# The maxima of a sliding-window attention, laid out in scratch as a transpose leaves them, with a new order of one unit's transfers

## Chip, cores and metric

The kernel runs on one NeuronCore of a Trainium2 chip. The metric is the device time of one execution in microseconds. The core has a matrix engine (PE, with its weight loads as PEld), a vector engine (DVE), a scalar engine (ACT), GpSimd (POOL) and a sync engine (SP) which here issues nearly all the DMA transfers. Each engine works through its own instructions in order; semaphores tie them to each other.

## What is computed

Two branches over the same input `x` (2048 tokens, 512 features, float32), mixed by a sigmoid gate per token:

```python
def _A_ref(x, wqkv, wo):          # H = 32 heads of 16, window W = 256
    q, k, v = ...                 # x @ wqkv, split in heads
    scores = einsum("bhqd,bhkd->bhqk", q, k) * (Dh ** -0.5)
    scores = where(0 <= query - key < W, scores, -1e9)
    p = softmax(scores, axis=-1)
    return einsum("bhqk,bhkd->bhqd", p, v)... @ wo

def _B_ref(x, w_gate, w_up, w_down):
    return (sigmoid(x @ w_gate) * (x @ w_up)) @ w_down

g = sigmoid((x * gate_w).sum(-1, keepdims=True))
return g * _A_ref(...) + (1 - g) * _B_ref(...)
```

## The kernel before

**Number format.** Every float32 operand is split in a high and a low part (ACT rounds the high one, DVE subtracts), and three products replace one.

**Units.** Heads go in 8 groups of 4, tokens in 16 blocks of 128; the main loop (line 779) runs over units u, one block of one head group each, 128 in all (`NU`), and a tail of ten more. Four units make a step s (512 tokens of a head group, 32 in all), two steps a stack t of the ring.

**The ring.** For scores the kernel keeps stacked operands in a ring of three (`ring`, line 101): per head 64 rows that hold the parts of q and of k, in four slots along the second axis: slots 0 and 1 for q (heads 0 and 1 of a group in slot 0, heads 2 and 3 in slot 1), slots 2 and 3 for k. Row 0 of each 32 is the place where -max of a query is put, as a high and a low part in two groups of rows, so that the second score product comes out with the maximum subtracted already. `stack_build` (line 281) lists a stack's transfers: a fill that puts zeros in the rows of the maxima, eight of the high parts (`ring<-sh`) and four of the low (`ring<-sl`). They are put on SP four at a time, in four units from u = 8k+1 on (`sdma[:SD]`, line 799).

**Two passes of scores.** In unit u, for each of the group's four heads, `s_part` (line 314) forms the scores with the queries on partitions, and DVE takes each query's masked maximum (`mxs`). `LAG` = 9 units later `st_part` (line 366) forms them again, transposed, with keys on partitions and the maximum subtracted; ACT takes the exponential into `pbuf`, and GpSimd masks it. `st` of unit u reads queries of up to two blocks ahead of block u-9.

**The maxima's way.** After the four units of a step DVE negates and splits the maxima (`max_split`, line 337) into `nm`, 128 queries on partitions by 32 columns (head, part, block), and transposes it in 32x32 squares into `nt`: partition (a, h, l, b), 32 columns t, where a is the quarter of the 128 queries. `max_store` (line 347) sends it to DRAM in four transfers, one for each a, so that the scratch is laid out (h, l, b, query); `max_load` (line 353) reads it into the ring with one transfer: four destination partitions, two slots, runs of 512 floats.

**Visits.** From u = 13 (`PVLAG`) on, every fourth unit is a visit: before its first scores, the product of the exponentials with the values (`pv_part`, line 400) of a finished step runs; six key blocks as a rule, four for the first step of a head group (u = 13, 29, 45, ...). In a visit step (u-5)//4 is also split and stored. ACT copies the product out (`o_take`, line 417) in the visit's first slot, and lists five stores of it: four to `oT_scratch`, one of the sums. Visits are at u = 13, 17, 21, ...; every second one (17, 25, ... 113) is also the unit in which a stack's transfers begin.

**Order on SP.** SP's order is the order of the program. At the start of a unit `run_dmas(later)` issues the stores listed before it, then up to four transfers of a stack go; in a visit the four stores of the maxima follow inside the unit. The load of the maxima comes in the unit after the visit (`u % 4 == 2`, line 803), behind that unit's `later` and its share of the stack. Loads of weights and stores of gate and up products (`gu_scratch<-sp`, by `later`) stand among these.

**Filler work and held projections.** Between the score products the matrix engine does the projections of q and k (`pj`), then the gate and up products (`gu`), by a generator of turns. ACT and DVE work that follows is kept in lists: `evac` (one a slot, first), `acts` (one a slot if `evac` is empty), `behind` (DVE). A finished projection is copied to a buffer (`pr`, from the same four buffers, tag `sp`, that the gate and up products are copied to) and its split is put in `held` until the unit that line 821 names.

Of the kernel before, what the change touches and what calls it, by code (L numbers as in the profile page):

```python
# [7 lines left out]
F32 = mybir.dt.float32  # L8
# [6 lines left out]
P = 128  # L15
# [5 lines left out]
HG = 4  # L21
NG = H // HG
CH = 512
NC = T // CH
# [15 lines left out]
PVLAG = LAG + 4  # L40
SD = 4
QB = 32
# [15 lines left out]
def gated_mix_kernel(  # L58
# [11 lines left out]
    nc = tc.nc  # L70
# [21 lines left out]
    rec_d = nc.dram_tensor("rec_scratch", (NC, H, CH), F32, kind="Internal").ap()  # L92
    gu_d = nc.dram_tensor("gu_scratch", (2, NFM, P, T), F32, kind="Internal").ap()
    tail_d = nc.dram_tensor("tail_scratch", (NB, P, 2 * TF), F32, kind="Internal").ap()
    max_d = nc.dram_tensor("max_scratch", (NG * NC, HG, 2, 4, P), F32, kind="Internal").ap()
    fill_d = nc.dram_tensor("fill_scratch", (2, CH2), F32, kind="Internal").ap()

    cpool = ctx.enter_context(tc.tile_pool(name="cpool", bufs=1))
# [14 lines left out]
    NU = NG * NB  # L113
# [22 lines left out]
    with ExitStack() as actx:  # L136
# [159 lines left out]
        def run_dmas(dmas):  # L296
            for dst, src in dmas:
                nc.sync.dma_start(dst, src)  # L298
# [36 lines left out]
        nms = {}  # L335

        def max_split(s):
            mx = mxs.pop(s)
            nm = spool.tile([P, HG, 2, 4], F32R, tag="nm", name=f"nm{s}", bufs=1)
            nc.vector.tensor_scalar(nm[:, :, 0], mx, -1.0, None, op0=ALU.mult)  # L340
            nc.vector.scalar_tensor_tensor(
                nm[:, :, 1], mx, -1.0, nm[:, :, 0].bitcast(F32), op0=ALU.mult, op1=ALU.subtract,
            )
            nms[s] = spool.tile([P, QB], F32, tag="nt", name=f"nt{s}")
            nc.vector.transpose(nms[s], nm.bitcast(F32).rearrange("p h l b -> p (h l b)"))

        def max_store(s):
            nt = nms.pop(s)
            dst = max_d[s].rearrange("h l b (a t) -> a (h l b) t", t=QB)
            for a in range(P // QB):  # L350
                nc.sync.dma_start(dst[a], nt[a * QB:(a + 1) * QB])

        def max_load(s):
            st = ring[s // 2 % RING].bitcast(F32).rearrange("(a r) j f -> r a j f", r=QB)
            o = s % 2 * CH
            nc.sync.dma_start(
                st[0, :, 0:2, o:o + CH], max_d[s].rearrange("(p s) l b t -> (s l) p (b t)", p=2),
            )

        homes = (((0, 1), (9, 1), (3, 2), (4, 2)), ((0, 1), (3, 1), (9, 2), (10, 2)))  # L360

# [33 lines left out]
        later = []  # L395
# [102 lines left out]
        def gu_mm(f, c, w, k, half=None, second=False):  # L498
            if (f, c, w) not in gp:
                gp[f, c, w] = ps.tile([P, CH], F32, tag="misc", name=f"gu{f}_{c}_{w}", bufs=3)  # L500
            return group_mm(gp[f, c, w], gv[:, 0, w], gv[:, 1, w], c, k, half, second)
# [51 lines left out]
        def proj_post(s):  # L553
            proj_hi(s)
            behind.append(lambda: proj_lo(s))
# [41 lines left out]
        def proj_sum(s):  # L597
# [12 lines left out]
                lambda k, h=None, x=False, a=(f, c, w): gu_mm(*a, k, h, x),  # L610
# [9 lines left out]
        held = []  # L620
# [139 lines left out]
        def hold_group(step, _, post):  # L760
            for k in range(3 * ND):
                step(k)
            post()
# [8 lines left out]
        sdma = []  # L772
# [6 lines left out]
        for u in range(N):  # L779
            if u == LAG:  # L780
                vctx.close()
                pctx = ExitStack()
                ppool = pctx.enter_context(tc.tile_pool(name="ppool", bufs=1))
                pbuf = ppool.tile([P, 15, HG, P], F32, name="pbuf")
                pv = ps.tile([P, CH], F32, tag="pv", name="pv", bufs=1)
            if u == 1:
                proj_post(NC)
            if u == 4:
                load_gu(0, 0)
                load_gu(0, 1)  # L790
            if u % 8 == 1 and u > 8 and u // 8 + 1 < NP:
                sdma = stack_build(u // 8 + 1)
            if u % 16 == 8 and u // 16 + 2 < NG:
                raw_q = load_wqk(u // 16 + 2)
            if u in (4, 8, NU):
                max_store(u // 4 - 1)
            run_dmas(later)
            later.clear()
            run_dmas(sdma[:SD])
            del sdma[:SD]  # L800
            if u in (5, LAG):
                max_load(u // 4 - 1)
            if u % 4 == 2 and PVLAG < u < NU:
                max_load(u // 4 - 1)
            if u in WD_LOAD:
                load_d(WD_LOAD[u])
            if u == NU:
                max_load(NSTEP - 1)
            if u in TAIL_LOAD:
                tail_load(TAIL_LOAD[u])  # L810
            if u == WO:
                both = apool.tile([P, ND, CH], F32, tag="w0", name="woraw")
                wo_raw.extend(both[:, d] for d in range(ND))
                nc.sync.dma_start(both, wo.rearrange("(c p) n -> p c n", p=P))
            for s4 in proj_at.get(u, ()):
                if u < LAG:
                    first.insert(0, (
                        lambda k, h, s4=s4: proj_slot(s4, k, h), lambda s4=s4: proj_sum(s4)))
                else:
                    work.append(proj_group(s4))  # L820
            while held and u >= 8 * (held[0][0] // 2) - 11:
                acts.append(held.pop(0)[1])
            if u == N - 1:
                hold_group(*rest.pop(0))
            for hh in range(HG):
                if hh == 0 and u >= PVLAG and (u - PVLAG) % 4 == 0:
                    pv_part((u - PVLAG) // 4)
                    if u < NU:
                        max_split((u - 5) // 4)
                        max_store((u - 5) // 4)  # L830
                if u < NU:
                    s_part(u, hh)
                if 0 <= u - LAG < NU:
                    st_part(u - LAG, hh ^ 1 if u < NU else hh)
                if u < LAG:
                    flush(behind)
                    if hh % 2 == 1:
                        upto = n_first * (2 * u + 1 + hh // 2) // (2 * LAG)
                        run_first(upto - done)
                        done = upto  # L840
                else:
                    dense = u < NU and (u - PVLAG) % 4 == 3 and hh > 0
                    if behind and not dense:
                        behind.pop(0)()
                    if evac:
                        evac.pop(0)()
                    elif acts and not dense and (u < NU or hh % 2 == 1):
                        acts.pop(0)()
                if u >= LAG and (hh % 2 == 1 or u < NU) and ((u - PVLAG) % 4 < 3 or hh < HG - 1):
                    if u < N - 2:  # L850
                        next(slots)
            if u < LAG:
                flush(soon)
            if u == LAG - 1:
                split_gu(0, 0)
                split_gu(0, 1)
            if u in (3, 7, NU - 1):
                max_split(u // 4)
            if u // 16 + 2 < NG:
                if u % 16 == 13:  # L860
                    acts.append(lambda g=u // 16 + 2, r=raw_q: (
                        split_wqk(g, r, 0), behind.append(lambda: split_wqk(g, r, 1))))
            if 0 <= u - LAG < NU:
                mask_p(u - LAG)
            if u in TAIL_SPLIT:
                acts.append(lambda d=TAIL_SPLIT[u]: tail_split(d))
            if WD_LOAD.get(u - 1, 8) < 8:
                acts.append(lambda f=WD_LOAD[u - 1]: split_d(f, True))
            if u in WO_SPLIT:
                acts.extend(lambda d=d: wo_split(d) for d in range(WO_SPLIT[u], WO_SPLIT[u] + 1))  # L870
            if SUMS <= u < N - 1 and (u - SUMS) % 4 == 0:
                sums_load((u - SUMS) // 4)
            if SUMS + 2 <= u and (u - SUMS) % 4 == 2:
                behind.append(lambda c=(u - SUMS) // 4: later.append(sums_invert(c)))
            if u == TREAD:
                tail_reads(0)
            if u >= TREAD:
                tail_read(0, 2)
            for n in H_LOAD.get(u, ()):
                h_load(n)  # L880
            if u == N - 1:
                pctx.close()
                lpool = actx.enter_context(tc.tile_pool(name="lpool", bufs=1))
                spare = [lpool.tile([P, CH], F32, name=f"spare{k}") for k in range(6)]
            if u >= N - 2:
                flush(evac)
                flush(acts)
                flush(behind)
                h_skew(u - N - 1)
# [49 lines left out]
        for n, (c, f) in enumerate(steps):  # L939
# [45 lines left out]
            for t in range(4):  # L985
                r = slice(t * QB, (t + 1) * QB)
                mm(pd[t], lw[r, c], w3[r], start=False, stop=True)
            for t in range(4):
                b = 4 * c + t
# [64 lines left out]
```

## Time and profile before

| | before |
|---|---|
| median of three runs | 805.75 us (804.4 to 807.63) |
| the profiled execution | 799.52 us, of which 797.8 are the span from its first to its last instruction |
| PE busy, of the span | 93% |
| DVE, ACT, POOL busy | 61%, 53%, 21% |
| granted PE clock, mean | 0.972 |
| DMA | 103.64 MB, 94607 packets, of them 44958 under 512 B |

The page is of one execution. Its group rows give line, engine, operation, output and inputs by tile name, count, then busy time, mean duration in ns, and the idle time of the engine before such instructions with what ended it. The timeline gives start, duration, engine, line, operation, and in brackets the idle time before; the DMA rows of SP give the time of the issue, not of the transfer. In the chain of waits a DMA's row runs from its issue to its landing.

### The profile page before, as it was taken

To read this page: it belongs to the slowest core of one execution; us is meant where nothing else is said; L and a number is where in the kernel's file an instruction comes from. 1 tells how busy PE (TensorE), PEld (TensorE's weight loads), DVE (VectorE), ACT (ScalarE), POOL (GpSimd) and SP (SyncE) were. 2 spreads that over 40 slices of the span, in tenths; PEclk is the share of its full clock that TensorE was granted. 3 is DMA by queue.
4 is the path that set the end of the run, shared out by engine and by line. 5 is a ranking of instruction groups with operands and counts; after the bars stand their busy time and mean duration, and the time that the engine had idled before them with its cause. 6 is when DMAs were issued, how large, how long until landed. Compare 5 with 4: busy or idle time off the path is not lost.

```text
span 797.8 us, 17545 instructions
## 1 busy us (share of the span) xinstructions
PE 744.7 (93%) x6298; PEld 614.8 (77%) x6298; DVE 487.9 (61%) x1455; ACT 424.3 (53%) x890; POOL 167.4 (21%) x255
## 2 busy tenths in 40 slices
PE   9999989898898979888798989879989999999998
PEld 7788868686787768777687778767878888888886
DVE  4388756565574656565465756655764676848481
ACT  5424746465574546555464656555547564535341
POOL 6101321232232223222221322232223100000000
PEclk9999999999999999999989999998999999999999
DMA  7342342433535233343424242534257797949451
GB/s 280 96 121 65 99 129 81 114 94 94 140 91 144 86 99 99 97 123 97 126 67 136 76 125 65 159 104 126 75 167 221 203 273 193 254 130 268 116 112 53
DMA packets 94607, 103.64 MB, mean 130 GB/s; under 512 B 44958, under 2 KB 57758, under 8 KB 94520
## 3 DMA queue, kind: packets, MB, share of 16 engines
q1 hardware_dynamic: 94376, 102.40, 45.9%
q8 instruction: 49, 0.80, 0.4%
q14 instruction: 38, 0.31, 0.1%
q10 hardware_dynamic: 144, 0.13, 0.0%
HBM read 45.32 MB, written 31.99 MB: 97 GB/s over the span
## 4 chain that ended last, share of the span: by engine, by line
PE 84%; SPq 7%; DMA 5%; issue 2%; ACT 1%; DVE 1%; DVEq 0%; ACTq 0%
PE gu L252 22%; PE pv L408 10%; PE pj L252 9%; PE s L324 6%; SPq L298 6%; PE tp L543 5%; PE st L373 5%; PE pd L86 5%; PE pd L88 5%; PE pd L87 5%; DMA ring<-max_scratch 4%; PE vh L580 3%; PE pa L86 2%; PE pa L87 2%; PE pa L88 2%; PE vps L446 2%
## 5 line engine op out<-in xcount | busy, mean ns | idle before, releaser
L330 DVE CUSTOM_DVE_ANT_0 junk<-s,mask 128x384 f32<-128x384 f32 (+2 forms) x512 | 271.9, 531 | 207.4 <-PE s L324 151.2
L378 ACT ACTIVATE pbuf<-st 128x384 f32<-128x384 f32 (+2 forms) x512 | 241.4, 477 | 232.1 <-PE st L373 168.1
L252 PE MATMUL gu<-xh,w 64*128 64x512 f32 x1152 | 292.3, 401 | 0.0
L373 PE MATMUL st<-ring 64*128 64x384 f32 (+2 forms) x536 | 173.0, 339 | 46.9 <-DMA ring<-max_scratch 46.9
L252 PE MATMUL gu<-xl,w 64*128 64x512 f32 x576 | 192.0, 399 | 0.0
L384 POOL TENSOR_SCALAR_AFFINE_SELECT pbuf<-pbuf 128x512 f32<-128x512 f32 x128 | 85.1, 665 | 437.5 <-ACT pbuf L378 396.4
L252 PEld LDWEIGHTS gu<-xh,w 64*128 64x128 f32 x1152 | 164.5, 190 | 10.4
L324 PE MATMUL s<-ring 64*128 64x384 f32 (+2 forms) x536 | 167.9, 331 | 0.7 <-DVE mx L330 0.6
L373 PEld LDWEIGHTS st<-ring 64*128 64x128 f32 x536 | 100.0, 192 | 57.3 <-issue 48.4
L324 PEld LDWEIGHTS s<-ring 64*128 64x128 f32 x536 | 98.2, 190 | 18.4 <-issue 4.5
L252 PEld LDWEIGHTS gu<-xl,w 64*128 64x128 f32 x576 | 94.2, 190 | 3.7
L252 PE MATMUL pj<-xh,wqh 64*128 64x512 f32 (+1 forms) x228 | 89.3, 418 | 0.0
L252 PE MATMUL pj<-xl,wqh 64*128 64x512 f32 (+1 forms) x228 | 89.0, 415 | 0.0
L408 PE MATMUL pv<-pbuf,V 128*32 128x384 f32 (+2 forms) x1408 | 84.3, 386 | 0.0
L252 PE MATMUL pj<-xh,wql 64*128 64x512 f32 (+1 forms) x228 | 76.4, 422 | 0.0
L408 PEld LDWEIGHTS pv<-pbuf,V 128*32 128x32 f32 x1408 | 41.5, 110 | 41.1 <-issue 30.7
L390 POOL TENSOR_SCALAR_AFFINE_SELECT pbuf<-pbuf 128x512 f32<-128x512 f32 x112 | 73.0, 652 | 0.0
L86 PE MATMUL pd<-ring,hb 128*128 128x512 f32 x160 | 62.3, 389 | 0.0
L88 PE MATMUL pd<-ring,hb 128*128 128x512 f32 x160 | 62.3, 389 | 0.0
L87 PE MATMUL pd<-ring,hb 128*128 128x512 f32 x160 | 62.2, 389 | 0.0
L82 ACT CAST hb<-V 128x512 fp32r<-128x512 f32 x40 | 24.9, 622 | 56.0 <-DVE V L744 47.8
L252 PEld LDWEIGHTS pj<-xh,wql 64*128 64x128 f32 (+1 forms) x228 | 45.6, 204 | 2.3
(127 smaller groups left out, 1122.9 us busy)
## 6 DMA issues: line engine op xcount, KB each, us to landing
gu_scratch<-sp SPq DMA_DIRECT2D x72, 256.0 KB
V<-gu_scratch SPq DMA_DIRECT2D x36, 512.0 KB
ring<-sh SPq DMA_DIRECT2D x128, 128.0 KB
ring<-sl SPq DMA_DIRECT2D x64, 128.0 KB
guraw<-in_wgu_dram SPq DMA_DIRECT2D x18, 256.0 KB
oT_scratch<-ob SPq DMA_DIRECT2D x128, 32.0 KB
xl<-oT_scratch SPq DMA_DIRECT2D x16, 256.0 KB
V<-in_xT_dram SPq DMA_DIRECT2D x15, 256.0 KB
```

Of the source, the lines that this page charges most:

```text
L86: mm(ps, lh, rh, start=first, stop=False)
L87: mm(ps, lh, rl, start=False, stop=False)
L88: mm(ps, ll, rh, start=False, stop=last)
L252: return mm(pt, (wl if w == 2 else wh)[r, d], (xl if w == 1 else xh)[r, d, c * CH:(c + 1) * CH], start=k == 0 and not second, stop=k == 3 ...
L298: nc.sync.dma_start(dst, src)
L324: mm(pt[:, (k - k0) * P:(e - k0) * P], lhsT, blk(g, k, hh, 1, e - k), start=k == k0, stop=e == i + 1, skip_group_check=True,)
L330: nc.vector.tensor_tensor_reduce(junk[:, 0:n], pt[:, 0:n], mask[:, 3 * P - n:], scale=1.0, scalar=NEG, op0=ALU.add, op1=ALU.max, accum_out ...
L373: mm(pt[:, (q - j) * P:(e - j) * P], lhsT, blk(g, q, hh, 0, e - q), start=q == j, stop=e == last, skip_group_check=True,)
L378: exps.append(nc.scalar.activation(p_blk(u, hh, 0, n), pt[:, 0:n * P].rearrange("p (b t) -> p b t", t=P), AF.Exp, scale=SCALE,))
L384: nc.gpsimd.affine_select(pbuf[:, s0], pbuf[:, s0], pattern=[[0, HG], [1, P]], compare_op=ALU.is_ge, fill=0.0, base=0, channel_multiplier=-1,)
L390: nc.gpsimd.affine_select(old, old, pattern=[[0, HG], [-1, P]], compare_op=ALU.is_gt, fill=0.0, base=0, channel_multiplier=1,)
L408: mm(pv[32 * hh:32 * hh + 32, (q - q0) * P:(e - q0) * P], Vf[:, v:v + 32], p_blk(g * NB + j, hh, q - j, e - q), start=j == j0, stop=j == q ...
```

## The change

The scratch of the maxima gets the transposed tile's own order, (a, h, l, b, t). The store is one transfer of 128 partitions. The load gathers the four quarters: two transfers, one for each of the two slots p, in runs of 32 floats. In a visit nothing is issued at the unit's start; after the split the listed stores go, then the store of the maxima, and ahead of the third head's scores (`hh == 2`) the stores listed since (the values among them), the load, and only then up to four transfers of the stack. The load at `u % 4 == 2` is gone. Held projections are split from unit 8t-10 on instead of 8t-11.

```diff
-    max_d = nc.dram_tensor("max_scratch", (NG * NC, HG, 2, 4, P), F32, kind="Internal").ap()
+    max_d = nc.dram_tensor("max_scratch", (NG * NC, P // QB, HG, 2, 4, QB), F32, kind="Internal").ap()
...
         def max_store(s):
-            nt = nms.pop(s)
-            dst = max_d[s].rearrange("h l b (a t) -> a (h l b) t", t=QB)
-            for a in range(P // QB):
-                nc.sync.dma_start(dst[a], nt[a * QB:(a + 1) * QB])
+            nc.sync.dma_start(max_d[s].rearrange("a h l b t -> (a h l b) t"), nms.pop(s))
 
         def max_load(s):
             st = ring[s // 2 % RING].bitcast(F32).rearrange("(a r) j f -> r a j f", r=QB)
             o = s % 2 * CH
-            nc.sync.dma_start(
-                st[0, :, 0:2, o:o + CH], max_d[s].rearrange("(p s) l b t -> (s l) p (b t)", p=2),
-            )
+            src = max_d[s].rearrange("a (p s) l b t -> p (s l) b a t", p=2)
+            for p in range(2):
+                nc.sync.dma_start(
+                    st[0, :, p, o:o + CH].rearrange("r (b a t) -> r b a t", b=4, a=P // QB), src[p],
+                )
...
-            run_dmas(later)
-            later.clear()
-            run_dmas(sdma[:SD])
-            del sdma[:SD]
+            visit = PVLAG <= u < NU and (u - PVLAG) % 4 == 0
+
+            def transfers():
+                run_dmas(later)
+                later.clear()
+                if visit:
+                    max_load((u - 5) // 4)
+                run_dmas(sdma[:SD])
+                del sdma[:SD]
+
+            if not visit:
+                transfers()
             if u in (5, LAG):
                 max_load(u // 4 - 1)
-            if u % 4 == 2 and PVLAG < u < NU:
-                max_load(u // 4 - 1)
...
-            while held and u >= 8 * (held[0][0] // 2) - 11:
+            while held and u >= 8 * (held[0][0] // 2) - 10:
                 acts.append(held.pop(0)[1])
...
                 if hh == 0 and u >= PVLAG and (u - PVLAG) % 4 == 0:
                     pv_part((u - PVLAG) // 4)
-                    if u < NU:
+                    if visit:
                         max_split((u - 5) // 4)
+                        run_dmas(later)
+                        later.clear()
                         max_store((u - 5) // 4)
+                if hh == 2 and visit:
+                    transfers()
```

## The prediction

> **What bounds the kernel now.** I read the page first: its engine table and its costliest groups.
>
> ```profile
> span 797.8 us, 17545 instructions
> PE 744.7 (93%) x6298; PEld 614.8 (77%) x6298; DVE 487.9 (61%) x1455; ACT 424.3 (53%) x890; POOL 167.4 (21%) x255
> L373 PE MATMUL st<-ring 64*128 64x384 f32 (+2 forms) x536 | 173.0, 339 | 46.9 <-DMA ring<-max_scratch 46.9
> ```
>
> TensorE is busy for 744.7 of 797.8 us, and 46.9 of the 53.1 idle microseconds end with the landing of the load of the maxima (line 356). Next the chain in order of time, and the table of stretches, cut for the thirteen visits that also send a stack (u = 17, 25, ... 113). First the unit u+1, then the unit u+2, each from its first `s` matmul to the next unit's (columns: stretch, length, busy time of each engine with its instructions, granted clock, DMA share, GB/s).
>
> ```profile
> 215.80 2.23 DMA ring<-max_scratch
> 218.03 0.14 issue
> ```
>
> ```profile
> sum 45.34, PE 45.34 PEld 39.51 DVE 31.06 ACT 32.15 POOL 16.00; mean PE 3.49 PEld 3.04 DVE 2.39 ACT 2.47 POOL 1.23
> ```
>
> ```profile
> 107.76:114.79 7.03, 3.75 (x34) 3.45 (x33) 2.13 (x9) 2.66 (x7) 1.22 (x2) 1.00 0.70 205
> 215.82:223.13 7.31, 5.29 (x34) 4.99 (x33) 2.68 (x10) 3.24 (x8) 1.22 (x2) 0.77 0.73 184
> ...
> 533.74:544.77 11.03, 5.11 (x34) 4.81 (x33) 2.11 (x9) 2.70 (x7) 1.22 (x2) 0.69 0.64 176
> sum 108.57, PE 64.64 PEld 60.77 DVE 29.68 ACT 31.18 POOL 15.88; mean PE 4.97 PEld 4.67 DVE 2.28 ACT 2.40 POOL 1.22
> ```
>
> The same 34 or so matmuls take 45.3 us in the thirteen units u+1 (PE busy throughout) and 108.6 us in the units u+2: **63.2 us are lost there**. 43.9 of them is waiting (108.57 - 64.64); the other 19.3 is PE running slowly afterwards, at a mean clock of 0.77 in the second row and 0.69 in the third (in a few stretches 1.00, as in the first). So a wait costs itself and usually some 1.8 us more (5.29 busy for what takes 3.49). Two other visits wait too, in the chain:
>
> ```profile
> 161.84 2.25 DMA ring<-max_scratch
> 587.09 2.15 DMA ring<-max_scratch
> ```
>
> At 161.84 (u = 29) only some 0.8 us of it is idle PE: 46.9 - 43.9 = 3.0 is left for the two, and the one at 587.09 (u = 125) takes 2.2. With a slow stretch behind the latter (1.8) that is 0.8 + 4.0. **All of it together: 63.2 + 0.8 + 4.0 = 68.0 us.**
>
> **Why the load is late.** SP's own queue in the timeline, a visit without a stack (u = 37) and one with (u = 41):
>
> ```profile
> 193.00 1.72 SPq L351 DMA_DIRECT2D max_scratch<-nt  x4
> 195.09 1.70 SPq L298 DMA_DIRECT2D oT_scratch<-ob  x4
> 196.83 0.56 SPq L298 DMA_DIRECT2D sum_scratch<-ob  x1
> 197.56 0.58 SPq L356 DMA_DIRECT2D ring<-max_scratch  x1
> ...
> 206.16 0.53 SPq L298 DMA_DIRECT2D ring<-fill_scratch  x1
> 206.74 1.80 SPq L298 DMA_DIRECT2D ring<-sh  x3
> 208.64 2.21 SPq L351 DMA_DIRECT2D max_scratch<-nt  x4
> 210.95 1.76 SPq L298 DMA_DIRECT2D oT_scratch<-ob  x4
> 212.76 0.55 SPq L298 DMA_DIRECT2D sum_scratch<-ob  x1
> 213.35 2.41 SPq L298 DMA_DIRECT2D ring<-sh  x4
> 215.80 0.58 SPq L356 DMA_DIRECT2D ring<-max_scratch  x1
> ```
>
> With the stack, SP never rests from 206.16 on: 0.53 + 1.80 of stack, the four stores, five value stores, 2.41 of stack, then the load. What it waits for and who waits for it (ACT's copy of the values, DVE's transpose, the first `s` matmul of both visits, two `st` matmuls of unit 39):
>
> ```profile
> 209.71 0.58 ACT L420 COPY ob<-pv 128x512 f32<-128x512 f32 x1
> 207.42 0.21 DVE L345 STREAM_TRANSPOSE nt<-nm 128x32 f32<-128x32 f32 x1
> 193.51 0.44 PE L324 MATMUL s<-ring 64*128 64x384 f32 x1
> 208.75 0.44 PE L324 MATMUL s<-ring 64*128 64x384 f32 x1
> 200.60 0.27 PE L373 MATMUL st<-ring 64*128 64x256 f32 x1
> 202.28 0.27 PE L373 MATMUL st<-ring 64*128 64x256 f32 x1
> ```
>
> Without the stack the load goes out 4.05 us after the visit's first `s`, with it 7.05. The reader is the first `st` of unit u+2: 200.60 behind u = 37, and just behind 215.82 (where the stretch above begins) behind u = 41, both 7.1 us after the first `s`. Only the stack visits and those whose PV product has four blocks (13, 29, ... 125) need it so early; for u = 21, 37, ... the maxima belong to a new head group, which `st` reaches two units later.
>
> **The change part by part.**
>
> *The store.* Three issues fewer: 3 x 0.42 plus gaps, 1.4 us of SP. The pieces stay 128 of 128 bytes. It waits for the transpose: at u = 41 it can go at 207.65 instead of 208.64, as the stack is no longer ahead of it.
>
> *The value stores* keep their wait: ACT's copy ends at 209.71 + 0.58 = 210.29, so they run 210.35 to 212.05 and the sums to 212.65. This, not the maxima, now sets the load. The store has been away for 5 us by then, so the load's wait for it is free.
>
> *The load* then goes at the place that the visit without a stack already shows, 4.05 us after the first `s`: 212.8 instead of 215.80. It is two issues now (0.58 + 0.05 more). The first half holds the rows of the first two `st` of a unit, the second half those of the last two, 1.7 us later (202.28 against 200.60).
>
> *Its pieces.* The maxima used to come in 8 runs of 2 KB; now each half is 64 runs of 128 bytes. No row shows such a transfer to four partitions. The nearest are the late reads of the tail scratch (line 709), also 128-byte runs, and the page's mean over all packets:
>
> ```profile
> 621.66 0.91 SPq L298 DMA_DIRECT2D xh<-tail_scratch  x2
> 622.69:623.89 1.20, 1.20 (x14) 0.84 (x16) 0.83 (x1) 1.19 (x2) 0.49 (x1) 1.00 0.74 121
> q1 hardware_dynamic: 94376, 102.40, 45.9%
> ```
>
> 121 GB/s for 1.20 us are 1134 runs, 71 on each of 16 engines: 17 ns a run. The page's mean is 0.459 x 16 x 797.8 / 94376 = 62 ns a packet. How many engines share a half isn't shown. Lower end: 64 runs over 16 engines at 17 ns, 0.07 us. Upper end: all on one engine at 62 ns, 4.0 us. I take 0.3 us, near the low end, because the runs of the first row have this very size, with room for fewer than 16 engines. The Trainium skill, "DMA: Bandwidth & Descriptors", section "Why a DMA increments its semaphore by 16 and not by 1", has the engine count as the largest number up to 16 that divides the slowest dimension of both sides: four here, which speaks against this layout (a 128-partition store gets 16) and would give 16 x 17 ns = 0.27 us; no row here shows the count.
>
> Issue to landing was 2.15 to 2.25 us in the rows above; with 0.3 more the first half lands at 212.8 + 2.55 = 215.35, and PE wants it at 215.7 (0.14 us before the `st`). **Slack 0.35 us**, so the wait is gone; the second half lands at 216.0 and is wanted at 217.4. The four-block visits run the same instructions behind their first `s`, so I give them the same figures: they don't wait either.
>
> *The stack* starts behind the load, at 214.0 instead of 206.2, four pieces there and four in each of the next units. Its first reader is unit u+7, over 20 us later: hidden. If that cover were gone it would cost its 4 x 0.6 us a visit, 31 us in all. Behind it on SP stand the stores of gate and up products that the visit's last two slots list; they go some 2.5 us later. Their readers come in the last stage, and their source is one of four buffers, asked for again four products on, over 10 us later: nothing.
>
> *The hold* lets ACT's cast and DVE's subtraction of a projection start a unit later (limit -10 instead of -11):
>
> ```profile
> L275 ACT CAST sh<-pr 128x512 fp32r<-128x512 f32 x27 | 17.0, 631 | 0.0
> ```
>
> 0.63 us each on an engine that is 53% busy, three units ahead of the stack that sends them: nothing. At worst a copy of the gate products waits for the buffer that the held projection still has, about 1.3 us (cast and subtraction) in each of 14 pairs.
>
> *What stays.* At u = 113 SP is held by another load ahead of the store:
>
> ```profile
> 529.24 0.62 DVE L536 TENSOR_TENSOR tail_wql<-tailraw,tail_wqh 128x450 fp32r<-128x450 f32 x1
> 529.89 0.33 SPq L522 DMA_DIRECT2D tailraw<-in_wgu_tail_dram  x1
> 579.19 0.42 SPq L814 DMA_DIRECT2D woraw<-in_wo_dram  x1
> 581.64 3.52 SPq L298 DMA_DIRECT2D oT_scratch<-ob  x4
> ```
>
> Store at 530.25, five value stores to 533.1, load at 533.2, landing 535.75; wanted at 533.7 (unit u+2 begins at 533.74). So 2.0 us of wait remain, and half the time a slow stretch: 2.9. (The Trainium skill, "TensorE: Matmul & The Clock Gate", Part 1, has the clock halved only after an idle window of about 3.4 us; here a 2.02 us wait at 215.8 was enough, the measurement decides. By the page this item would be 2.0.) At u = 125 the 1 MB load of `wo` still stands ahead and stretches the value stores (3.52 for four, else 1.76): about 1.2 + 0.4. Single issues are late now and then:
>
> ```profile
> L351 SPq DMA_DIRECT2D max_scratch<-nt x128: 309/419/1720, 53.7 to 596.8; - x128
> ```
>
> The longest took 1.72 us where 0.42 is the median; for such I keep 2.5 us over the other 19 early visits.
>
> **Sum:** 68.0 - 2.9 - 1.6 - 2.5 = 61 us gained. The profiled execution took 799.5 us (span 797.8 and 1.7 around it): 738.5. It was 6.2 us below the median of the runs shown; whether that distance belongs to the waits (they would be gone) or not, I can't tell, and take half: **742 us**.
>
> **Rivals.**
> 1. *The first reader waits for both halves.* The kernel keeps one ring tensor, so the dependency may cover the whole. Then the landing is 0.63 later, 0.3 us past the need, or 1.0 past it with 16 runs at 62 ns: 6 to 20 us over 20 early visits, 748 to 762. For it: the old load was one transfer for all. Against: the halves are disjoint rows. Chance 0.15.
> 2. *A new wait on ACT* by the held buffers, 14 x 1.3 = 18 us: 760. Against: ACT's idle share. 0.08.
> 3. *The small runs take the place of the wait* (slower). All 64 runs of a half go one after another at 62 ns: 4.0 us a half. In 20 early visits, six of which wait for nothing today, the first half is then 3.4 us late and the second 2.3 more; with 1.8 of slow clock, 7.5 x 20 = 150 us, for the 68 saved: 880. It decides from about 2 us a half (then 20 waits of some 1.6 us and the clock make the 68). Against: the 17 ns row. 0.04.
> 4. *It doesn't do what it says:* something else holds SP in front of the load and the time stays. Against: the visits without a stack, whose load goes at 4.05 us. 0.03.
>
> **How the numbers follow.** Forecast 0.70, rivals 0.15, 0.08, 0.04, 0.03. The forecast's own end below is every wait gone, 799.5 - 68.0 = 731.5; rivals 1 and 2 reach 762 and with the 6.2 us a little over. Range 732 to 766. A change within 0.5% (4 us) is about what this measurement can't tell from none: faster 0.93, same 0.02, slower 0.05.
>
> **What would show it.** In the new profile: the idle time of the `st` group falls from 46.9 to under 6 us; the clock stays at 1.00 behind nearly all visits; SP shows store, five value stores, two loads, stack in that order, the first load about 4 us after the visit's first `s`; PE's busy time falls by some 20 us, since its slow matmuls go. Wrong would be: waits on the load in most stack visits (rival 1 or 3, told apart by their length), ACT waiting at L505, or the first load later than 5 us.

## The result and the profile after

| | before | after |
|---|---|---|
| median of six runs | 803.57 us (799.8 to 807.63) | 737.14 us (735.82 to 738.5) |
| the profiled execution, and its span | 799.52, 797.8 us | 737.48, 735.8 us |
| PE idle in the span | 53.1 us | 10.9 us |
| granted PE clock, mean | 0.972 | 0.999 |

The ratio after / before is **0.9172 [0.9141, 0.9204]**. From the page of after, the head of its engine table and two groups (busy time, mean ns | idle time before, and what ended most of it):

```profile
span 735.8 us, 17513 instructions
PE 724.9 (99%) x6298; PEld 591.0 (80%) x6298; DVE 488.4 (66%) x1455; ACT 423.5 (58%) x890; POOL 167.0 (23%) x255
...
L372 PE MATMUL st<-ring 64*128 64x384 f32 (+2 forms) x536 | 167.7, 329 | 4.1 <-DMA ring<-max_scratch 2.8
...
L504 ACT COPY sp<-gu 128x512 f32<-128x512 f32 x72 | 42.2, 586 | 3.9 <-DMA gu_scratch<-sp 3.9
```

The load of the maxima ended 46.9 us of idle PE before; it ends 2.8 now. PE's busy time fell by 19.8 us as well (744.7 to 724.9), with the same 6298 matmuls: these ran at a lower granted clock before.

The table of stretches of after, over the same thirteen units u+2 (u = 17, 25, ... 113; stretch, length, busy time of each engine, granted clock, DMA share, GB/s):

```profile
202.29:205.78 3.49, 3.49 (x35) 2.96 (x33) 2.57 (x10) 3.12 (x8) 1.22 (x2) 1.00 0.78 195
...
481.03:486.49 5.46, 3.75 (x34) 3.45 (x33) 2.13 (x9) 2.67 (x7) 1.22 (x2) 1.00 0.44 99
sum 47.48, PE 45.77 PEld 40.43 DVE 30.42 ACT 31.75 POOL 15.88; mean PE 3.52 PEld 3.11 DVE 2.34 ACT 2.44 POOL 1.22
```

108.57 us became 47.48: **61.1 of the 62.0 us that the span lost**. u = 41, which took 7.31 us at a clock of 0.77, takes 3.49 at 1.00; only u = 113 is still long. The rest, from the first `s` of a unit to that of the next: from unit 127 to the end 211.53 became 207.67 us (3.9 gained), unit 109 went from 3.60 to 5.29 (1.7 lost), unit 31 from 4.29 to 4.95 (0.7 lost), and small differences lose 0.6.

SP in the timeline of after, at u = 41 (first `s` at 195.21; an issue's start and duration):

```profile
194.12 0.32 SPq L348 DMA_DIRECT2D max_scratch<-nt  x1
196.78 1.71 SPq L298 DMA_DIRECT2D oT_scratch<-ob  x4
198.53 0.55 SPq L298 DMA_DIRECT2D sum_scratch<-ob  x1
199.19 1.14 SPq L355 DMA_DIRECT2D ring<-max_scratch  x2
200.37 0.50 SPq L298 DMA_DIRECT2D ring<-fill_scratch  x1
200.93 5.01 SPq L298 DMA_DIRECT2D ring<-sh  x8
```

Store, five value stores, two loads, then the stack; the first load goes 3.98 us behind the first `s` (7.05 before). The store goes before the visit's first `s`, SP is idle until ACT's copy of the values, and the stack keeps SP busy only after the load has gone.

**Where time is still lost.** First u = 113, SP and then one row of the chain of waits:

```profile
477.18 0.33 SPq L521 DMA_DIRECT2D tailraw<-in_wgu_tail_dram  x1
...
478.05 0.42 SPq L348 DMA_DIRECT2D max_scratch<-nt  x1
...
481.08 1.14 SPq L355 DMA_DIRECT2D ring<-max_scratch  x2
```

```profile
481.08 1.86 DMA ring<-max_scratch
```

The load of the tail's weights holds SP until 477.18, 3.1 us behind the first `s` (474.10) and 5.0 after the maxima are transposed. (That nothing is issued at a visit's start holds for the stores and the stack only: loads of weights still go there, at u = 109, 113 and 125.) The load of the maxima goes at 481.08 and PE waits 1.71 us for it, with no slow stretch behind (clock 1.00 in the last row of the table of stretches). The second wait (1.1 us) is in unit 31, behind u = 29, where the last transfers of a stack stand ahead of the store on SP:

```profile
146.96 2.54 SPq L298 DMA_DIRECT2D ring<-sl  x4
149.59 1.35 SPq L348 DMA_DIRECT2D max_scratch<-nt  x1
...
153.85 1.21 SPq L355 DMA_DIRECT2D ring<-max_scratch  x2
```

The third loss is new and isn't a wait for the maxima. SP and ACT around unit 109 (first `s` at 456.52), and the chain:

```profile
449.88 4.29 SPq L298 DMA_DIRECT2D ring<-sh  x5
454.21 1.87 SPq L298 DMA_DIRECT2D ring<-sl  x3
456.18 0.53 SPq L298 DMA_DIRECT2D gu_scratch<-sp  x1
```

```profile
458.93 0.58 ACT L504 COPY sp<-gu 128x512 f32<-128x512 f32 x1 [3.87 <-DMA gu_scratch<-sp]
```

```profile
456.18 2.67 DMA gu_scratch<-sp
```

The store of gate products at 456.18 stands behind eight transfers of the stack. Its buffer is wanted again by ACT's next copy, which waits 3.87 us for the landing; the next exponential stands behind that copy on ACT, and the unit takes 1.7 us longer.

### The profile page after: what moved, and what is told of

The parts are those of the page before. It is cut to its first block, busy times and chain, and to the rows that moved or that the text cites. A ratio compares the mean times of both kernels' runs of the same rounds, so it can differ in the third digit from the quotient of the medians.

```text
span 735.8 us, 17513 instructions
## 1 busy us (share of the span) xinstructions
PE 724.9 (99%) x6298; PEld 591.0 (80%) x6298; DVE 488.4 (66%) x1455; ACT 423.5 (58%) x890; POOL 167.0 (23%) x255
## 4 chain that ended last, share of the span: by engine, by line
PE 93%; DMA 2%; SPq 2%; issue 1%; DVE 1%; ACT 1%; DVEq 0%; ACTq 0%
PE gu L252 26%; PE pv L407 11%; PE pj L252 10%; PE s L324 6%; PE st L372 5%; PE tp L542 5%; PE pd L87 5%; PE pd L86 5%; PE pd L88 5%; PE vh L579 3%; PE pa L86 2%; PE pa L88 2%; PE pa L87 2%; SPq L298 2%; PE vps L445 2%
## 5 line engine op out<-in xcount | busy, mean ns | idle before, releaser
L252 PE MATMUL gu<-xh,w 64*128 64x512 f32 x1152 | 282.4, 393 | 0.0
L252 PE MATMUL gu<-xl,w 64*128 64x512 f32 x576 | 186.8, 391 | 0.0
L372 PE MATMUL st<-ring 64*128 64x384 f32 (+2 forms) x536 | 167.7, 329 | 4.1 <-DMA ring<-max_scratch 2.8
L252 PEld LDWEIGHTS gu<-xh,w 64*128 64x128 f32 x1152 | 156.9, 185 | 11.6
L324 PEld LDWEIGHTS s<-ring 64*128 64x128 f32 x536 | 94.9, 184 | 22.5 <-DVE mx L330 7.2
L372 PEld LDWEIGHTS st<-ring 64*128 64x128 f32 x536 | 96.1, 184 | 11.9 <-ACT pbuf L377 2.3
L252 PEld LDWEIGHTS gu<-xl,w 64*128 64x128 f32 x576 | 90.5, 185 | 3.7
L252 PE MATMUL pj<-xl,wqh 64*128 64x512 f32 (+1 forms) x228 | 83.1, 392 | 0.0
L252 PE MATMUL pj<-xh,wqh 64*128 64x512 f32 (+1 forms) x228 | 83.0, 393 | 0.0
L252 PE MATMUL pj<-xh,wql 64*128 64x512 f32 (+1 forms) x228 | 70.5, 393 | 0.0
L504 ACT COPY sp<-gu 128x512 f32<-128x512 f32 x72 | 42.2, 586 | 3.9 <-DMA gu_scratch<-sp 3.9
```

What stands on the lines that cost most here:

```text
L252: return mm(pt, (wl if w == 2 else wh)[r, d], (xl if w == 1 else xh)[r, d, c * CH:(c + 1) * CH], start=k == 0 and not second, stop=k == 3 ...
L324: mm(pt[:, (k - k0) * P:(e - k0) * P], lhsT, blk(g, k, hh, 1, e - k), start=k == k0, stop=e == i + 1, skip_group_check=True,)
L372: mm(pt[:, (q - j) * P:(e - j) * P], lhsT, blk(g, q, hh, 0, e - q), start=q == j, stop=e == last, skip_group_check=True,)
L504: nc.scalar.copy(t, gp.pop((f, c, w)))
```

## The experiments

Each ratio is to before as it was measured beside that kernel (medians of 802.57 to 805.83 us).

| kernel | median us | ratio to before, 95% |
|---|---|---|
| before (of the case) | 803.57 | 1 |
| after | 737.14 | 0.9172 [0.9141, 0.9204] |
| order_only | 742.44 | 0.9225 [0.9184, 0.9266] |
| layout_only | 777.01 | 0.9659 [0.9600, 0.9718] |
| stack_first | 763.05 | 0.9472 [0.9423, 0.9522] |
| hold_11 | 739.95 | 0.9199 [0.9151, 0.9248] |
| halves_swapped | 739.78 | 0.9189 [0.9145, 0.9232] |
| load_first | 735.62 | 0.9147 [0.9106, 0.9187] |
| tail_later | 733.53 | 0.9116 [0.9077, 0.9154] |
| load_first_tail | 731.12 | 0.9088 [0.9049, 0.9128] |
| stack_by_three | 770.73 | 0.9611 [0.9583, 0.9639] |
| best_by_three | 779.71 | 0.9734 [0.9686, 0.9781] |

### The two halves of the change: order_only and layout_only

order_only is after with the old scratch, the four stores and the one load; layout_only is before with the new scratch, store and loads, and nothing else.

```diff
-            nc.sync.dma_start(max_d[s].rearrange("a h l b t -> (a h l b) t"), nms.pop(s))
+            nt = nms.pop(s)
+            dst = max_d[s].rearrange("h l b (a t) -> a (h l b) t", t=QB)
+            for a in range(P // QB):
+                nc.sync.dma_start(dst[a], nt[a * QB:(a + 1) * QB])
...
-            src = max_d[s].rearrange("a (p s) l b t -> p (s l) b a t", p=2)
-            for p in range(2):
-                nc.sync.dma_start(
-                    st[0, :, p, o:o + CH].rearrange("r (b a t) -> r b a t", b=4, a=P // QB), src[p],
-                )
+            nc.sync.dma_start(
+                st[0, :, 0:2, o:o + CH], max_d[s].rearrange("(p s) l b t -> (s l) p (b t)", p=2),
+            )
```

For layout_only the same lines are exchanged the other way, in the kernel before.

> The changed kernel's order and hold with the scratch, the four stores and the single load of the kernel before. Theory (order): the waits went because the load no longer stands behind the stack; the layout gives next to nothing. The four stores start at the transpose (1.1 to 1.9 us ahead of the visit's first s in stack visits) and are out before the values are copied (1.55 us behind it), so the single load goes at about 4 us and lands 2.15 us later, 0.7 us ahead of the need: 735 to 740 us, under 6 us of waits on the load. Rival (layout): SP lacks the 1.4 us a visit that the three issues took, the load comes over 1 us late in most of the 20 early visits: 750 to 770 us.

> The kernel before with the new scratch alone: one store, two loads, everything else in the old order. Theory (order): SP reaches the first load 1.4 us sooner in the thirteen stack visits, whose waits shrink by 1.4 us each but stay (most are 2 to 4.6 us): 18 us and some slow clock less, 775 to 790 us. Rival (layout): the issues saved were the larger part: under 760 us.

**Measured:** 742.44 us, 2 us above the theory's range and far from the rival's, and 777.01, inside its range. Who waits for the load, from the table of waits (total us, times, longest), first order_only, then layout_only:

```profile
PE st L373 <- DMA ring<-max_scratch: 5.9, 3, 3.6
```

```profile
PE st L372 <- DMA ring<-max_scratch: 30.9, 14, 4.7
```

The order alone takes off 62.9 us (805.34, the before of these runs, less 742.44); the layout alone 28.3; both 66.4 (803.57 less 737.14). They don't add up because both pull at one thing, the time at which SP reaches the load: three issues fewer help wherever the load is late, and behind the new order it is late almost nowhere. Of what the layout still gives there (3.9 us between the spans, 5.3 between the medians) 3.4 us are in the unit behind u = 113. SP of order_only at that place:

```profile
477.61 0.33 SPq L522 DMA_DIRECT2D tailraw<-in_wgu_tail_dram  x1
...
478.87 1.81 SPq L351 DMA_DIRECT2D max_scratch<-nt  x4
480.73 1.81 SPq L298 DMA_DIRECT2D oT_scratch<-ob  x4
...
483.29 0.55 SPq L356 DMA_DIRECT2D ring<-max_scratch  x1
```

Four stores behind the blocked load of the tail cost 1.81 us instead of 0.42. PE waits 3.64 us instead of 1.71, and now the clock drops behind the wait: unit 115 takes 8.88 us instead of 5.46.

### The stack ahead of the load: stack_first

```diff
             def transfers():
                 run_dmas(later)
                 later.clear()
+                run_dmas(sdma[:SD])
+                del sdma[:SD]
                 if visit:
                     max_load((u - 5) // 4)
-                run_dmas(sdma[:SD])
-                del sdma[:SD]
```

> The changed kernel with one exchange: in a visit the four transfers of the stack go ahead of the load instead of behind it, still inside the visit. Theory (order): the load goes out 2.4 us later in the thirteen stack visits, at about 6.4 us behind the first s, lands at 8.3 and is wanted at 6.95: 1.4 us of wait each, 18 us, 753 to 760 us, and more if the clock drops behind such waits (up to 780 us). Rival (only the earlier unit and the layout count): 736 to 742 us.

**Measured:** 763.05 us, a little above the range. SP at u = 41 (first `s` at 198.76), and the waits:

```profile
202.73 0.53 SPq L298 DMA_DIRECT2D ring<-fill_scratch  x1
203.31 1.81 SPq L298 DMA_DIRECT2D ring<-sh  x3
205.16 1.15 SPq L355 DMA_DIRECT2D ring<-max_scratch  x2
```

```profile
PE st L372 <- DMA ring<-max_scratch: 22.7, 13, 4.9
```

Four issues ahead of the load move it from 4.0 to 6.4 us (the first half), and all thirteen stack visits wait again, eleven of them by 1.2 to 2.0 us. So **the position of the load on SP's queue, not the amount of data, made the wait**: the same transfers, in another order, are worth 26 us between the medians.

### The order of the two halves: halves_swapped

```diff
-            for p in range(2):
+            for p in (1, 0):
```

> The changed kernel with the second half of the load (heads 2 and 3) issued ahead of the first. The half that PE wants first then leaves at 4.6 us behind the visit's first s instead of 4.0. Theory (short runs are cheap, the slack is large): it lands by 6.4 to 6.9 us, wanted at 6.95 to 7.1; only the few late visits (25, 29, 77, 109, 113) lose some 0.6 us each: 737 to 741 us. Rival (the slack was 0.35 us, as I had worked out): a wait of 0.3 us in nearly all of the 20 early visits, 742 to 745 us.

**Measured:** 739.78 us, and in the waits:

```profile
PE st L372 <- DMA ring<-max_scratch: 4.1, 4, 2.3
```

Units 31, 99, 111 and 115 wait, that is u = 29, 97, 109 and 113 (and u = 25 by 0.15 us), though the half that is wanted first now goes 0.6 us later everywhere. Of the five that the theory named 77 doesn't wait, and 97 was not named. So the slack at the usual visits is over 0.6 us, not the 0.35 of the prediction. In after itself the reader doesn't wait for both halves: at u = 25 the second half is issued at 138.33 us and, by the updates of its semaphore in the trace, lands at 140.14; the first `st` of unit 27 runs at 139.67.

### The later hold: hold_11

```diff
-            while held and u >= 8 * (held[0][0] // 2) - 10:
+            while held and u >= 8 * (held[0][0] // 2) - 11:
```

> The changed kernel with held projections split from unit 8t-11 on, as before. Theory: the hold is worth nothing, 735 to 740 us. Rival: the casts in the visit at u = 13, 21, 29, ... delay the copy of the values and so the load, by 0.6 us or more in the seven four-block visits: 741 us or more.

**Measured:** 739.95 us; its interval overlaps that of after, so the time alone tells no difference. The profile does. DVE and SP of hold_11 at u = 29 (first `s` at 146.11):

```profile
150.97 1.10 DVE L279 TENSOR_TENSOR sl<-pr,sh 128x512 fp32r<-128x512 f32 x1 [2.07 <-DMA ring<-sl]
```

```profile
145.59 2.50 SPq L298 DMA_DIRECT2D ring<-sl  x4
```

The split of the next projection writes into the staging buffers from which the stack before is sent (two of them), and finds them still being read. DVE works in order, so the next maxima stand behind the split, and unit 30 takes 5.61 us instead of 3.48; units 46, 54 and 78 lose 0.6 to 1.1 likewise (there too the split starts 0.1 to 0.2 us after a `ring<-sl` has landed), and some others gain. In after no such wait is left; the shortest distance from that landing to the split is 1.9 us, in unit 31. A unit lasts some 3.5 us or more, so **the hold's one unit is the cover for the stack's later issue**. What it is worth in time these runs don't tell.

### Where SP goes on losing time: load_first, tail_later, load_first_tail

```diff
                     if visit:
-                        max_load((u - 5) // 4)
...
                         max_store((u - 5) // 4)
+                        max_load((u - 5) // 4)
```

```diff
-TAIL_LOAD = {109: 0, 111: 1, 113: 2, 114: 3}
+TAIL_LOAD = {109: 0, 111: 1, 114: 2, 115: 3}
```

The first is load_first, the second tail_later; load_first_tail has both.

> The changed kernel with the load right behind the store, ahead of the value stores. SP waits for the store's landing (1.4 us) in the time in which it waits for ACT's copy of the values now. Theory (the values set the load's place, not the maxima): in an ordinary visit nothing is gained, as nothing waits; at u = 113 the load goes 1.5 us sooner and the wait of 1.7 us shrinks to about 0.3; 29, 77 and 109 lose their remainder: 731 to 736 us. Rival: the value stores and the stack behind the waiting load come later and ACT or PE waits for them: 738 us or more.

> The changed kernel with the third and fourth load of the tail weights one unit later (units 114 and 115 instead of 113 and 114), so that no blocked load stands ahead of the store in the visit of unit 113. Theory: its wait (1.7 us, unit u+2 of 5.5 instead of 3.5 us) goes: 734 to 736 us. Rival: the load's block only moves and holds the stack or the gate stores instead: 737 us or more.

> Both of these, the load right behind the store and the two tail loads one unit later. If the two losses are separate: 730 to 735 us, PE idle for under 8 us of the span. If they are the same one: as load_first.

**Measured:** 735.62, 733.53 and **731.12 us**. SP at u = 113, first load_first, then load_first_tail:

```profile
473.73 0.42 SPq L348 DMA_DIRECT2D max_scratch<-nt  x1
476.56 1.14 SPq L355 DMA_DIRECT2D ring<-max_scratch  x2
477.75 1.84 SPq L298 DMA_DIRECT2D oT_scratch<-ob  x4
```

```profile
468.24 0.32 SPq L348 DMA_DIRECT2D max_scratch<-nt  x1
469.69 1.14 SPq L355 DMA_DIRECT2D ring<-max_scratch  x2
471.68 2.66 SPq L298 DMA_DIRECT2D oT_scratch<-ob  x4
```

load_first lets the load overtake the value stores. At 113 it gains little: the store is still held by the tail's load, and the load waits on SP for the store's landing (476.56 behind 473.73). A wait of 1.5 us stays (0.3 was expected), and what stands behind the load is late in its turn: unit 118 takes 5.30 us instead of 3.48, with a new wait on ACT:

```profile
ACT tail_hb L534 <- DMA ring<-sl: 3.1, 2, 2.5
```

At 29 and 109 both losses of after are gone (units 31 and 109 take 3.60 and 3.57). tail_later takes the tail's load out of unit 113, and unit 115 takes 3.48 us. Together no wait for the load remains. load_first alone isn't told from after by the times (the intervals overlap). load_first_tail lies below after's whole interval and has **the lowest median here, ahead of both kernels of the case**; its interval overlaps that of tail_later.

### Fewer transfers at a time: stack_by_three, best_by_three

```diff
-SD = 4
+SD = 3
```

> The changed kernel with three instead of four transfers of a stack in a unit (five units instead of four). At unit 109 of the changed kernel ACT waits 3.9 us for a buffer whose store stood behind eleven transfers of a stack on SP, and that unit takes 5.3 instead of 3.6 us. Theory (the stack, moved behind the load, holds the gate stores that are listed later): with three a unit the stores come in between, the wait at 109 goes: 734 to 737 us. Rival (the last transfers of the stack only slide into the next visit and hold its store): 738 us or more, with the loads of units 29, 45, 77 later than now.

> The fastest so far (load behind the store, tail loads a unit later) with three transfers of a stack in a unit. It has no wait on the load left, so the theory gives no change, 730 to 733 us; the rival (the stack slides into the next visit) 733 us or more.

**Measured:** 770.73 us (after with three) and 779.71 (load_first_tail with three). Both theories missed. The times lie in the open ranges of the rivals, and the stack does slide into the next visit, but little of the loss is what they name (a store or a load of the maxima that comes later). What the theory was about came in part: unit 109 takes 3.58 us, and ACT's wait for the gate store there is 1.6 us instead of 3.9. Three rows of stack_by_three's waits were not foreseen:

```profile
PEld s L324 <- DVE mx L330: 34.7, 41, 4.6
PE s L324 <- DVE mx L330: 20.6, 14, 4.1
DVE sl L279 <- DMA ring<-sl: 13.4, 6, 2.5
```

At u = 29 (first `s` at 150.75) the cause can be read across three engines. In order: SP, DVE, PE, and the chain of waits:

```profile
156.60 1.18 SPq L355 DMA_DIRECT2D ring<-max_scratch  x2
157.84 0.52 SPq L298 DMA_DIRECT2D ring<-sl  x1
```

```profile
160.58 0.69 DVE L279 TENSOR_TENSOR sl<-pr,sh 128x512 fp32r<-128x512 f32 x1 [2.48 <-DMA ring<-sl]
```

```profile
161.80 0.44 PE L324 MATMUL s<-ring 64*128 64x384 f32 x1 [1.26 <-DVE mx L330]
```

```profile
157.84 2.62 DMA ring<-sl
```

Thirteen transfers, three at a time, need five units instead of four: the last one falls into the next visit, behind that visit's load. DVE's next split wants its staging buffer, waits 2.48 us for the landing, holds the maxima, and so PE's score buffers: unit 31 takes 6.14 us. This is hold_11's mechanism, now in spite of the later hold. The row of `sl` names the DMA for six splits; by the semaphores in the trace eleven splits start, after an idle DVE, within 0.3 us of the landing of a `ring<-sl`, and the units in which they run lose 22.5 us against after. That is most of the 32.1 us by which the span grew; 3.5 more are in unit 119, where ACT's `tail_hb` waits for such a landing, and 2.5 in unit 115, the one that waits longer for the load (2.67 us). In best_by_three the row is 21.1 us in eight waits; why its stack lands later still isn't worked out.

## Why the prediction was right, point by point

- **What was lost, and what comes back.** The 63.2 us of the thirteen units came back but for u = 113: 61.1. Waiting and slow clock went together, as the sum had it (PE's busy time fell by 19.8 us, 19.3 of slow clock foreseen in these units).
- **The load's place.** ACT's copy of the values now sets it, as foreseen: 3.98 us at u = 41 for 4.05 predicted. Where the store is late (u = 29, 109, 113) SP sets it, at 6.4 to 7.1 us.
- **The small runs.** 0.3 us more were put down. This term had the wrong sign. The load of after landed 1.86 and 2.09 us after its issue in the two rows of its chain, and the old one 2.05 to 2.40 in thirteen of the fifteen rows of its own, 2.99 and 3.46 in two; a half has half the bytes, and its short runs cost nothing that can be seen. At u = 41 the first half, with 1.86 us to land, is there at 201.05; 0.14 ahead of the first `st` of unit 43 is 202.15. The slack was 1.1 us, not 0.35. By the Trainium skill ("DMA: Bandwidth & Descriptors", section "Why a DMA increments its semaphore by 16 and not by 1") only four engines would share such a half. The semaphore updates in the traces fit: besides one about 1 us after the issue, four come at the landing of a half and four at that of the old load, which went to four partitions too; the store has sixteen. So the layout left this count as it was, and it did not speak against the change.
- **u = 113.** 2.0 us of wait were to stay, with 0.9 for the clock: 1.71 stayed and the clock held 1.00, and unit 115 lost 2.0 in all (5.46 for 3.49). This term was 0.9 us too large.
- **u = 125.** 1.6 us were to stay, since the load of `wo` would still stand ahead and stretch the value stores. This step failed: the wait there, 2.58 us before, is gone. A store listed earlier, for which SP had to wait, is now issued inside the visit, so `wo` goes well ahead of it (514.78), and the value stores take 1.71 us, not 3.52:

```profile
514.78 0.39 SPq L819 DMA_DIRECT2D woraw<-in_wo_dram  x1
520.13 0.33 SPq L298 DMA_DIRECT2D tail_scratch<-tt  x1
521.51 0.33 SPq L348 DMA_DIRECT2D max_scratch<-nt  x1
522.94 1.71 SPq L298 DMA_DIRECT2D oT_scratch<-ob  x4
```

- **Late issues, 2.5 us.** They came to 3.8, and for the most part not by single late issues. 1.7 us of unit 109 come from a term that I had set at nothing (the stores of gate products behind the stack, "asked for again over 10 us later"). Unit 31 is 1.5 off: the wait at u = 29 was to give 0.8 us back (it was 0.44 us, with 2.58 at u = 125, where I had put 0.8 and 2.2), and it grew to 1.1, which costs 0.7. The small differences are 0.6.
- **The stack "hidden", the hold "nothing".** Right for this kernel, for an incomplete reason. I named only the ring's reader, over 20 us away. The nearer claimant is the next writer of the staging buffers, in the units just behind the stack's last transfers. hold_11 and the two kernels with three transfers show it: the later hold, which I priced as a possible cost, is what covers it.
- **The sum.** 738.5 us foreseen for the profiled execution, 737.48 measured: 61 us of gain against 62.0. That it is so near is luck in part, since the misses at u = 113 and 125 (0.9 and 1.5 too little) stand against the late issues (1.3 too much). The forecast of 742 lies 4.9 us above the median; 3.1 of it is half of the 6.2 us between profile and median before, which I carried over, and 0.4 is rounding. After, the two agree within 0.4 us: the distance went with the waits. That their length changes from run to run is the likely cause, not shown: six runs spread over 7.8 us before and 2.7 after.
- **The rivals.** The reader doesn't wait for both halves (rival 1: halves_swapped and u = 25). ACT waits for one of the four buffers in one place, not in fourteen, and there for a store, not for a held projection (rival 2). Small runs are not serial (rival 3); order and layout each do what they say (rival 4).

## What to carry to other kernels

When an engine waits for a DMA, read the whole queue of the engine that issues it: here 26 us hung on four issues of half a microsecond ahead of a transfer wanted sooner (stack_first), and 62.9 on the whole order (order_only). Before you call a transfer hidden, look for two claimants of its time, the reader of what it writes and the next writer of the buffer that it reads; the second was much the nearer here. Two savings in one queue don't add up once the transfer is in time: order and layout alone gave 62.9 and 28.3 us, and 66.4 together.

## What the runs showed of the hardware

**The clock can drop behind waits of about 2 us, and not at a sharp length.** Before, a wait of 1.84 us (u = 65) was followed by a slow stretch, and those of 2.93, 3.11 and 3.28 us (u = 105, 97 and 17) were not. In stack_first eleven waits of 1.17 to 1.98 us had none, the longest of them in this row of its table of stretches (unit 27: 5.73 us for 3.75 of PE, clock 1.00):

```profile
140.51:146.24 5.73, 3.75 (x34) 3.44 (x33) 2.11 (x9) 1.82 (x5) 1.23 (x2) 1.00 0.74 202
```

In layout_only one of 2.07 us had it and one of 2.22 hadn't; in halves_swapped one of 2.27 had. The Trainium skill ("TensorE: Matmul & The Clock Gate", Part 1) has the clock halved after an idle window of about 3.4 us, and says that this window runs freely. The runs agree that equal waits can end differently, but the drop came here behind PE waits a good deal shorter than such a window.

**A store of 16 KB does not always land after the same time.** In load_first_tail the store of the maxima at u = 113 lets the load go 1.45 us after its issue; in load_first, where the tail's load and a gate store had gone just ahead of it, 2.83 us. That these two are the cause is likely, but this one pair doesn't show it.
